# Attention scores by whole 128-key products instead of 64-key halves, with the work around them reordered

## The chip, the cores and the metric

The kernel runs on one core of one Trainium2 chip. The metric is device time in microseconds (us) of one launch. Engines are named as the profile names them: PE is the matrix engine and PEld its weight loads, DVE the vector engine, ACT the scalar engine, POOL the general engine, SP the one that issues most DMA transfers.

## The reference

A linear attention with a decay per key dimension (4 batches, 8 heads, 768 steps, head size 48) is followed by a mixture of experts in which some tokens keep the expert of the token before them.

```python
for t in range(S):                       # attention, all batches and heads at once
    cur = einsum('bhd,bhe->bhde', u * k[t], v[t])
    y[t] = einsum('bhd,bhde->bhe', r[t], state + cur)
    state = w[..., None] * state + einsum('bhd,bhe->bhde', k[t], v[t])
...
x = y.transpose(0, 2, 1, 3).reshape(B, S, H * D)          # B=4, S=768, H*D=384
logits, local_gate = x @ w_gate, sigmoid(x @ w_local)     # 8 experts
for b in range(B):
    for s in range(S):
        e = argmax(logits[b, s]) if s == 0 or local_gate[b, s] < 0.5 else prev_e
        prev_e = e
        out[b, s] = softmax(logits[b, s])[e] * (relu(x[b, s] @ w1[e]) @ w2[e])   # F = 1024
```

## The kernel before

The attention is done in 16 items, numbered n: a batch and a pair of heads each, with the two heads of a pair on partitions 0 to 47 and 64 to 111. The 768 steps of an item are six chunks of 128. The terms of an item are:

- `scale` (POOL): `ke`, keys scaled to the end of their chunk; `rw`, decayed receptances; `pd`, the products of receptance and key that the own term (`u`) needs. `keys` (DVE): `kw`, keys divided by the decay.
- `added` (PE): what each chunk adds to the state, into `mp`; `states` (DVE): the scan over chunks, `S`.
- `scores` (PE): keys times receptances within a chunk, three chunks in one PSUM pair of banks (`pair`, of which there are two, taken in turn by `banks`). Each call gives back the DVE product with a mask that writes `am`.
- `own` (PE, then one DVE product with `vT`): the own terms, which open the PSUM tile `y`. `inside` (PE) adds `am` times values to `y`, `before` (PE) adds what the state carries in. ACT then copies `y` to `xT`.
- `turn` (PE transposes, ACT copies): `xT` to token order in `x`, which is written to DRAM after the fourth pair of a batch. `logits` (PE, ACT) and `token_logits` (PE, ACT) follow once a batch, at n = 4, 8, 12 and at n = 5, 9, 13.

The order on each engine is the order of the program, written out by hand in `run` (a manual schedule); the framework adds only the semaphores. One pass of the loop in `run` for item n first turns item n - 2, makes keys, added states and scan of item n, issues POOL's work for item n + 1, finishes item n - 1 with `inside` and `before`, and then starts item n with `scores` and `own`. PE takes its instructions in that order, so an instruction that waits holds up all behind it. The tile `y` has one buffer: `own` of item n may not write it until `before` of item n - 1 is copied out. Of the two pairs of banks, `scores`, `logits`, `turn` and `token_logits` each take the next one, and wait until its last reader is done.

From n = 9 on the routing of the first two batches (`Router`, on DVE with a few PE products and ACT copies) is spread over the same loop; g is 8. What other engines take from it on the way: `router.keys` (PE) reads what `experts_of` wrote, `router.counts` (PE) what `one_hot` wrote, `router.summed` (PE) what `places` and `numbers` wrote.

The scores before are cut in half by keys: for one chunk and head there are two products with 64 keys each, one with all 128 receptances and one, for the later keys, with the last 64 alone. They go to different halves of the array and of the PSUM partitions, and odd chunks swap the halves, so the tokens of odd chunks are stored with swapped halves by the host (`_tokens`) and masked with a swapped mask (`kept`); `ends` and `turn_ends` hold both orders. The mask product of the second half of the scores is kept back: `run` calls it (`keep()`) behind `own`, except at n = 4, 8, 12, where it comes ahead of it.

The experts follow from about 116 us on. They are not touched, but for the name of a buffer whose memory they take over (`hs`).

Of the kernel before, what the change touches and what calls it, by code (L numbers as in the profile page):

```python
# [61 lines left out]
class Attention:  # L62
# [12 lines left out]

    def __init__(self, tc, st, rk_d, kv_d, vT_d, x_d, w_t, wp_d, kept, ident, lt, mp):
        self.tc, self.nc = tc, tc.nc
        nc = tc.nc
        self.rk_d, self.kv_d, self.vT_d, self.x_d = rk_d, kv_d, vT_d, x_d
        self.w_t, self.kept, self.ident, self.lt = w_t, kept, ident, lt  # L80

# [57 lines left out]

        self.end = once.tile([P, HP, P + DP], F32, name="end")  # L140
        self.endT = once.tile([P, 2, HP, 2 * DH], F32, name="endT")
        self.align(26)
# [23 lines left out]
    def ends(self, z):  # L166
        self.nc.scalar.copy(self.end[:, z, :P], self.tab[:, z, 0, P - 1::-1])
        self.nc.scalar.copy(self.end[:, z, P:], self.tab[:, z, 0, P - 1:DP - 1:-1])  # L168

    def turn_ends(self, z):  # L170
        ep, n = self.banks("ep"), z.stop - z.start
        for k in range(n):
            for o in range(2):
                self.nc.tensor.transpose(ep[:, o, k * P:(k + 1) * P], self.end[:, z.start + k, o * DP:o * DP + P], self.ident)
        self.nc.scalar.copy(self.endT[:, :, z].rearrange("p o i (h d) -> p o (i h) d", h=2),
                            ep[:, :, :n * P].rearrange("p o (i d) -> p o i d", d=DP)[..., :DH])

# [30 lines left out]
    def scale(self, n):  # L208

        nc, t = self.nc, self.items[n]  # L210
        t["ke"] = self.two.tile([P, NCH, 2 * DH], F32, name="ke")
        t["pd"] = self.two.tile([P, NCH, P], F32, name="pd")
        t["rw"] = self.three.tile([P, NCH, P], F32, name="rw")
        hp = t["hp"]

        def ke(p):
            nc.gpsimd.tensor_mul(t["ke"][:, p::2], t["k"][:, p::2], spread(self.endT[:, p, hp], 1, C2))  # L217

        def pd(i):
            z = slice(i * C2, (i + 1) * C2)  # L220
            nc.gpsimd.tensor_mul(t["pd"][:, z], t["rT"][:, z], t["kT"][:, z])  # L221

        def rw(i):
            self.decayed(nc.gpsimd, n, slice(i * C2, (i + 1) * C2))


        for what in (ke, rw, pd) if n > 2 else (pd, ke):
            for i in range(2):
                what(i)
# [32 lines left out]
    def own(self, n):  # L262

        nc, t = self.nc, self.items[n]
        t["y"] = y = self.py.tile([P, 2, 512], F32, name="y")
        for p in range(2):
            for h in range(2):
                q = slice(h * DP, h * DP + DH)
                nc.tensor.matmul(y[p * DP:(p + 1) * DP, h, :C2 * P].rearrange("p (c t) -> p c t", c=C2),
                                 lhsT=self.w_t[q, t["hp"], 1:2].to_broadcast([DH, DP]),  # L270
                                 rhs=t["pd"][q].rearrange("p (c k) t -> p k c t", k=2)[:, p],
                                 start=True, stop=True)
        nc.vector.tensor_mul(y[:, :, :C2 * P], y[:, :, :C2 * P], t["vT"].rearrange("p h c t -> p h (c t)"))

    def scores(self, n, g):
# [5 lines left out]
        for i in range(3):  # L281
            c = 3 * g + i
            for o in range(2):
                for h in range(2):
                    q, f = slice(h * DP, h * DP + DH), c % 2 ^ o

                    x = o * DP if n else 0
                    nc.tensor.matmul(sc[f * DP:(f + 1) * DP, h, i, x:], lhsT=t["kw"][q, c, o * DP:(o + 1) * DP],  # L288
                                     rhs=t["rw"][q, c, x:], start=True, stop=True)
        return lambda: nc.vector.tensor_mul(t["am"][:, g], sc, spread(self.kept[:, g:g + 3], 1, 2))  # L290

    def inside(self, n):
        nc, t = self.nc, self.items[n]
        for c in range(NCH):
            p, c2 = c % 2, c // 2
            for h in range(2):
                nc.tensor.matmul(t["y"][p * DP:(p + 1) * DP, h, c2 * P:(c2 + 1) * P],  # L297
                                 lhsT=t["v"][:, (2 * c + h) * DH:(2 * c + h) * DH + DP],
                                 rhs=t["am"][:, c // 3, h, c % 3], start=False, stop=False, skip_group_check=True)

    def before(self, n):
        nc, t = self.nc, self.items[n]
        if t["hp"] == 0:
            self.xTs[t["b"]] = self.late.tile([P, H, C2 * P], F32, name="xT")
            self.xs[t["b"]] = self.late.tile([P, NCH, D], F32, name="x", bufs=2)
        for c in range(1, NCH):
            p, c2 = c % 2, c // 2
            for h in range(2):
                q = slice(h * DP, h * DP + DH)
                nc.tensor.matmul(t["y"][p * DP:p * DP + DH, h, c2 * P:(c2 + 1) * P],  # L310
                                 lhsT=t["S"][q, :, c - 1], rhs=t["rw"][q, c],
                                 start=False, stop=True, skip_group_check=True)
        for h in range(2) if n == B * HP - 1 else (slice(0, 2),):
            (nc.vector.tensor_copy if h == 1 else nc.scalar.copy)(  # L314
                self.xTs[t["b"]][:, 2 * t["hp"]:2 * t["hp"] + 2][:, h], t["y"][:, h, :C2 * P])

    def turn(self, n, banks):

        nc, b, h0 = self.nc, self.items[n]["b"], 2 * self.items[n]["hp"]
        xT, x = self.xTs[b], self.xs[b]  # L320
        for h in range(2):
            for c2 in range(C2):
                nc.tensor.transpose(banks[h][:, c2 * P:c2 * P + U], xT[:U, h0 + h, c2 * P:(c2 + 1) * P], self.ident[:U, :U])
        for h in range(2):
            nc.scalar.copy(x[:, :, (h0 + h) * DH:(h0 + h + 1) * DH],
                           banks[h][:, :C2 * P].rearrange("p (c e) -> p c e", e=DP)[..., :DH])
        if h0 == H - 2:
            nc.scalar.dma_start(out=self.x_d[b * S:(b + 1) * S, :].rearrange("(c p) d -> p c d", p=P), in_=x)

    def logits(self, b, bank):  # L330
# [3 lines left out]
        for h in range(H):  # L334
            j = h % 4
            nc.tensor.matmul(bank[32 * j:32 * j + 32, :C2 * P], lhsT=self.wp[:, h], rhs=xT[:, h], start=(h < 4), stop=(h >= 4))
        nc.scalar.copy(lT, bank[:, :C2 * P])
# [7 lines left out]
    def run(self, router, fetch, heads):  # L345
# [11 lines left out]
        for n in range(M + 1):  # L357
# [71 lines left out]
            if n == g + 6:  # L429
                router.numbers(0)  # L430
            if n == M:
                router.shares(0)
# [19 lines left out]
            self.scores(n, 0)()  # L452
            keep = self.scores(n, 1)
            if n == g + 1:
                router.experts_of(0, (1,))
            if n == g + 3:
                router.one_hot(0, (1,))
            if n == g + 5:
                router.places(0, 0)
            if n == g + 6:  # L460
                router.places(0, 1)
            if n % HP == 0:

                keep()
                self.own(n)
                self.logits(n // HP - 1, pair("lp")[0])
                if n == g + 4:
                    router.ranks(0, (1,))
            else:
                self.own(n)  # L470
                keep()
            if n == g + 2:
# [4 lines left out]
def general_attention(tc, rk_d, kv_d, wu, wg_d, x_d, ident, lt):  # L477

    nc = tc.nc
    with tc.tile_pool(name="g1", bufs=1) as g1, tc.tile_pool(name="g2", bufs=2) as g2, \  # L480
# [4 lines left out]
        for i in range(2):  # L485
            nc.vector.memset(ones[i * DP:(i + 1) * DP, i:i + 1], 1.0)
        turned = g1.tile([P, P], F32, name="g_turned")
        nc.vector.tensor_copy(turned[:, :DP], ident[:, DP:])
        nc.vector.tensor_copy(turned[:, DP:], ident[:, :DP])
        with tc.For_i(0, HP, 1) as hp:  # L490
            wu_t = g1.tile([P, 2], F32, name="g_wu")
            nc.sync.dma_start(out=wu_t, in_=wu[bass.ds(hp, 1)].rearrange("o p x -> (o p) x"))
            with tc.For_i(0, B, 1) as b:
# [11 lines left out]
                for e in range(DH):  # L505
                    vp = gps.tile([P, 2, 512], F32, name="g_vp")
                    for c in range(NCH):
                        for i in range(2):
                            nc.tensor.matmul(
                                vp[i * DP:(i + 1) * DP, c // 3, (c % 3) * P:(c % 3 + 1) * P],  # L510
                                lhsT=v_t[:, c, i, e:e + 1].to_broadcast([P, DP]),
                                rhs=turned if c % 2 else ident,
                                start=True, stop=True)
# [451 lines left out]
class Experts:  # L965
# [397 lines left out]
    def run(self, att, flag, ready):  # L1363
# [40 lines left out]
        for i in range(n):  # L1404
# [3 lines left out]
            if i == EARLY:  # L1408
                self.fetch(i + 1, self.nc.sync)
                self.hs = self.spare.tile([P, 2, 3, BLOCKS[0] // 2], F32, name="hs", tag="xT")  # L1410
            if u["eleven"]:
# [150 lines left out]
def kernel(  # L1562
# [25 lines left out]

    kept = keep.tile([P, 4, P], F32, name="kept")
    lo, hi = slice(0, DP), slice(DP, P)  # L1590
    nc.gpsimd.tensor_copy(kept[:, 0], mask)
    nc.gpsimd.memset(kept[lo, 1, lo], 0.0)
    nc.gpsimd.tensor_copy(kept[lo, 1, hi], mask[lo, lo])
    nc.gpsimd.tensor_copy(kept[hi, 1, lo], mask[hi, hi])
    nc.gpsimd.memset(kept[hi, 1, hi], 1.0)
    nc.scalar.copy(kept[:, 2:], kept[:, :2])
    lt = keep.tile([P, NC, E + 1], F32, name="lt")
# [6 lines left out]
    with ExitStack() as st, tc.manual_schedule():  # L1604
# [3 lines left out]
        ex = Experts(tc, st, x_d, w1, w2, out, ident, router)  # L1608
        att = Attention(tc, st, rk_d, kv_d, vT_d, x_d, w_t, wp_d, kept, ident, lt, router.mp)
        att.run(router, lambda: ex.fetch(0, nc.sync), lambda: ex.gather(0))  # L1610
# [52 lines left out]
def _tokens(a, np):  # L1663

    x = a.reshape(B, HP, 2, NCH, 2, DP, DH)
    x = np.stack([x[:, :, :, c, ::-1 if c % 2 else 1] for c in range(NCH)], 2)
    return x.transpose(0, 1, 4, 5, 2, 3, 6).reshape(B, HP, P, NCH * 2 * DH)

# [36 lines left out]
```

## Time and profile before

| what | value |
|---|---|
| three runs | 387.30, 389.34, 390.62 us; median 389.34 |
| the profiled execution | 388.15 us, with a span of 386.4 us |
| granted clock of PE | 0.997 |
| busy share of the span | PE 96%, PEld 85%, DVE 64%, POOL 39%, ACT 28% |
| instructions | PE 3858 products and as many loads, DVE 718, ACT 293, POOL 212 |
| attention | first scores at 7.45 us, last carried-in products at 115.53 us |
| mask products (L290) | 32 of 952 ns |
| DMA | 74.97 MB, mean 194 GB/s |

The span runs from the first to the last instruction; 1.75 us of the execution lie around it. A row of a timeline gives the start, the time from the first start to the last end of the instructions it gathers, the engine, the line, the operation, out<-in, the shape and the count, and in brackets the idle time of that engine just before with what ended it ("issue" where the profile shows nothing that it waited for). Each product of 32-bit values is recorded as two products and two loads. PE's starts are measured, its ends are modelled.

### The profile page before, as it was taken

The numbers are of one execution on the slowest core, as the hardware profiler recorded it, in microseconds if no ns is written. First come the engines' busy times: TensorE is split into PE (matmuls) and PEld (weight loads), VectorE is DVE, ScalarE is ACT, GpSimd is POOL, SyncE is SP. The second block draws the span as 40 slices with busy tenths as digits, with TensorE's granted clock in tenths as the row PEclk, the third lists the DMA queues.
The fourth block names the chain that finished last, engine by engine and source line by source line (L and its number), as shares of the span: only waits on it lengthen the run. The fifth ranks groups of instructions, "written<-read, shape, count | busy, mean of one in ns | idle before, by whom it ended". The sixth has DMA issues, their size and how long they took to land. (4 is left out here: it accounts for less than half of the span.)

```text
span 386.4 us, 9723 instructions
## 1 busy us (share of the span) xinstructions
PE 371.5 (96%) x3858; PEld 328.5 (85%) x3858; DVE 247.1 (64%) x718; ACT 107.6 (28%) x293; POOL 151.1 (39%) x212
## 2 busy tenths in 40 slices
PE   7999999799999999999999999999999999999992
PEld 6776877677777999998999999999999999999971
DVE  7887576588954564587657757758757758556400
ACT  4132232222213111322323233234224234222220
POOL 8769998696322022611333222312403213012022
PEclk9999999999999999999999999999999999999998
DMA  7999998979213982740552145245156146064011
GB/s 257 414 409 410 409 405 274 355 256 394 99 32 101 378 338 64 249 185 23 184 179 108 42 170 213 66 171 204 56 185 224 38 165 227 21 199 181 2 37 37
DMA packets 17477, 74.97 MB, mean 194 GB/s; under 512 B 2729, under 2 KB 6586, under 8 KB 14864
## 3 DMA queue, kind: packets, MB, share of 16 engines
q1 hardware_dynamic: 10048, 56.89, 39.1%
q0 software_dynamic: 3424, 9.52, 7.4%
q10 hardware_dynamic: 3952, 7.87, 5.6%
q8 instruction: 32, 0.52, 0.6%
q14 instruction: 21, 0.17, 0.1%
HBM read 64.83 MB, written 9.51 MB: 192 GB/s over the span
## 5 line engine op out<-in xcount | busy, mean ns | idle before, releaser
L1263 POOL DMA_INDIRECT out_dram<-yo,sid x27 | 26.6, 986 | 102.3 <-ACT yo L1258 78.8
L1114 PE MATMUL h<-exT,w1t 128*128 128x168 f32 (+4 forms) x240 | 54.9, 327 | 0.0
L1118 DVE TENSOR_TENSOR hT<-h,hs 128x168 f32<-128x168 f32 (+3 forms) x60 | 21.1, 351 | 46.5 <-PE h L1114 30.4
L1037 POOL DMA_INDIRECT xg<-x_d,gid x29 | 31.1, 1073 | 38.2 <-DVE sm L872 17.4
L1114 PEld LDWEIGHTS h<-exT,w1t 128*128 128x128 f32 x240 | 41.7, 190 | 0.3 <-issue 0.3
L290 DVE TENSOR_TENSOR am<-pair,kept 128x768 f32<-128x768 f32 x32 | 30.1, 952 | 16.8 <-PE pair L288 16.4
L1064 PE MATMUL h<-exT,w1t 128*128 128x192 f32 (+1 forms) x192 | 38.2, 337 | 0.0
L1183 PE MATMUL y<-factors,sums 128*128 128x192 f32 x168 | 36.8, 326 | 0.0
L1114 PE MATMUL h<-xs,ws 128*128 128x168 f32 (+4 forms) x144 | 35.2, 326 | 0.0
L1064 PEld LDWEIGHTS h<-exT,w1t 128*128 128x128 f32 x192 | 32.3, 190 | 1.4 <-issue 0.2
L221 POOL TENSOR_TENSOR pd<-rk 128x384 f32<-128x384 f32 x32 | 31.9, 1017 | 3.0 <-DMA rk<-in_rk_dram 2.2
L297 PE MATMUL y<-am,kv 128*64 128x128 f32 x384 | 28.9, 278 | 3.4 <-issue 2.2
L1114 PEld LDWEIGHTS h<-xs,ws 128*128 128x128 f32 x144 | 25.5, 190 | 4.3 <-ACT hs L1121 1.2
L1183 PEld LDWEIGHTS y<-factors,sums 128*128 128x128 f32 x168 | 28.9, 190 | 0.0
L297 PEld LDWEIGHTS y<-am,kv 128*64 128x64 f32 x384 | 24.8, 136 | 4.7 <-issue 2.4
L234 POOL TENSOR_TENSOR rw<-rk,tab 128x384 f32<-128x384 f32 x26 | 23.6, 931 | 7.3 <-PE y L310 7.3
L217 POOL TENSOR_TENSOR ke<-kv,endT 128x288 f32<-128x288 f32 x32 | 24.9, 799 | 3.9 <-DMA kv<-in_kv_dram 3.0
L314 ACT COPY xT<-y 128x768 f32<-128x768 f32 (+1 forms) x16 | 12.5, 779 | 42.3 <-PE y L310 42.3
L288 PE MATMUL pair<-rw,kw 48*64 48x128 f32 (+1 forms) x768 | 22.4, 249 | 1.3 <-ACT end L168 0.6
L1183 PE MATMUL y<-w2t,hT 128*128 128x192 f32 x96 | 23.0, 328 | 0.0
L1051 DVE COPY exT<-tp 128x384 f32<-128x384 f32 (+6 forms) x29 | 14.0, 489 | 12.8 <-PE tp L1050 12.6
L288 PEld LDWEIGHTS pair<-rw,kw 48*64 48x64 f32 x768 | 19.4, 133 | 2.7 <-issue 0.9
(279 smaller groups left out, 733.0 us busy)
## 6 DMA issues: line engine op xcount, KB each, us to landing
w1t<-in_w_dram SPq DMA_DIRECT2D x9, 1536.0 KB, 6.7
w2t<-in_w_dram SPq DMA_DIRECT2D x9, 1536.0 KB, 7.3
rk<-in_rk_dram SPq DMA_DIRECT2D x15, 768.0 KB, 9.4
kv<-in_kv_dram SPq DMA_DIRECT2D x16, 584.0 KB, 9.1
vT<-in_vT_dram SPq DMA_DIRECT2D x16, 384.0 KB, 7.4
x_d<-x ACTq DMA_DIRECT2D x4, 1152.0 KB, 10.7
w1t<-in_w_dram ACTq DMA_DIRECT2D x1, 1536.0 KB, 10.2
w2t<-in_w_dram ACTq DMA_DIRECT2D x1, 1536.0 KB, 13.5
```

The lines of the kernel that those rows point to most:

```text
L217: nc.gpsimd.tensor_mul(t["ke"][:, p::2], t["k"][:, p::2], spread(self.endT[:, p, hp], 1, C2))
L221: nc.gpsimd.tensor_mul(t["pd"][:, z], t["rT"][:, z], t["kT"][:, z])
L234: engine.tensor_mul(t["rw"][:, z], t["rT"][:, z], spread(pw, 1, z.stop - z.start))
L288: nc.tensor.matmul(sc[f * DP:(f + 1) * DP, h, i, x:], lhsT=t["kw"][q, c, o * DP:(o + 1) * DP], rhs=t["rw"][q, c, x:], start=True, stop=True)
L290: return lambda: nc.vector.tensor_mul(t["am"][:, g], sc, spread(self.kept[:, g:g + 3], 1, 2))
L297: nc.tensor.matmul(t["y"][p * DP:(p + 1) * DP, h, c2 * P:(c2 + 1) * P], lhsT=t["v"][:, (2 * c + h) * DH:(2 * c + h) * DH + DP], rhs=t["am" ...
L1037: self.nc.gpsimd.indirect_dma_start(out=xg[:n], out_offset=None, in_=self.x_d[:rows], in_offset=bass.IndirectOffsetOnAxis(ap=u["gid"][:n, ...
L1064: nc.tensor.matmul(h[:, :n], lhsT=u["w1"][:, m, kk, :], rhs=u["xT"][:, kk, :], start=(kk == 0), stop=(kk == DK - 1))
L1114: nc.tensor.matmul(out, lhsT=a, rhs=b, start=start and k == 0, stop=stop and k == len(terms) - 1, skip_group_check=True)
L1118: nc.vector.tensor_tensor(out, a, b, op=Alu.add)
L1183: return lambda: nc.tensor.matmul(bank[:, x * half:(x + 1) * half], lhsT=a, rhs=b, start=(j == 0 and x == 0), stop=(j == FK // 2 - 1), ski ...
L1263: self.nc.gpsimd.indirect_dma_start(out=out.rearrange("n (h d) -> (n h) d", h=2) if half else out, out_offset=bass.IndirectOffsetOnAxis(ap ...
```

## The change

1. **Scores.** For a chunk and a head there is one product: 128 keys by 128 receptances. The array is then used as two halves by rows (the two heads) in place of four quarters. The swapped order, `kept` and the second order of `end` and `endT` go; the mask is broadcast over three chunks and two heads.
2. **Order of an item from n = 3 on.** `scores` first half and its mask product, `own`, `scores` second half and its mask product, then `logits` where it is due. Items 0 to 2 keep their order.
3. **One tile a head.** `y` becomes `y0` and `y1`, `xT` becomes `xT0` and `xT1`. `own` goes through the heads outside and the halves inside, and its DVE product becomes two, one a head. The copy of `y` to `xT` is now split for every item: head 0 by ACT, head 1 by DVE (before, only the last item did this).
4. **Routing.** `experts_of` (second part, n = 9), `one_hot` (second part, n = 11) and `places` come behind the second mask product; before, they stood between the second scores and `own`, which on DVE is between the first mask product and the product of `own`. `places` of the first half moves from n = 13 to n = 14, and that of the second half from n = 14 to n = 15, there ahead of `inside`.

```diff
@@ own
-        t["y"] = y = self.py.tile([P, 2, 512], F32, name="y")
-        for p in range(2):
-            for h in range(2):
+        t["y"] = y = [self.py.tile([P, 512], F32, name=f"y{h}") for h in range(2)]
+        for h in range(2):
+            for p in range(2):
...
-        nc.vector.tensor_mul(y[:, :, :C2 * P], y[:, :, :C2 * P], t["vT"].rearrange("p h c t -> p h (c t)"))
+        for h in range(2):
+            nc.vector.tensor_mul(y[h][:, :C2 * P], y[h][:, :C2 * P], t["vT"][:, h].rearrange("p c t -> p (c t)"))
@@ scores
-            for o in range(2):
-                for h in range(2):
-                    q, f = slice(h * DP, h * DP + DH), c % 2 ^ o
-                    x = o * DP if n else 0
-                    nc.tensor.matmul(sc[f * DP:(f + 1) * DP, h, i, x:], lhsT=t["kw"][q, c, o * DP:(o + 1) * DP],
-                                     rhs=t["rw"][q, c, x:], start=True, stop=True)
-        return lambda: nc.vector.tensor_mul(t["am"][:, g], sc, spread(self.kept[:, g:g + 3], 1, 2))
+            for h in range(2):
+                q = slice(h * DP, h * DP + DH)
+                nc.tensor.matmul(sc[:, h, i], lhsT=t["kw"][q, c], rhs=t["rw"][q, c], start=True, stop=True)
+        return lambda: nc.vector.tensor_mul(t["am"][:, g], sc, spread(spread(self.mask, 1, 3), 1, 2))
@@ before
-        for h in range(2) if n == B * HP - 1 else (slice(0, 2),):
+        for h in range(2):
             (nc.vector.tensor_copy if h == 1 else nc.scalar.copy)(
-                self.xTs[t["b"]][:, 2 * t["hp"]:2 * t["hp"] + 2][:, h], t["y"][:, h, :C2 * P])
+                self.xTs[t["b"]][h][:, t["hp"]], t["y"][h][:, :C2 * P])
@@ run
             if n == g + 6:
                 router.numbers(0)
+            if n == g + 7:
+                router.places(0, 1)
...
             self.scores(n, 0)()
-            keep = self.scores(n, 1)
+            self.own(n)
+            self.scores(n, 1)()
+            if n % HP == 0:
+                self.logits(n // HP - 1, pair("lp")[0])
             if n == g + 1:
                 router.experts_of(0, (1,))
             if n == g + 3:
                 router.one_hot(0, (1,))
-            if n == g + 5:
+            if n == g + 4:
+                router.ranks(0, (1,))
+            if n == g + 6:
                 router.places(0, 0)
-            if n == g + 6:
-                router.places(0, 1)
-            if n % HP == 0:
-                keep()
-                self.own(n)
-                self.logits(n // HP - 1, pair("lp")[0])
-                if n == g + 4:
-                    router.ranks(0, (1,))
-            else:
-                self.own(n)
-                keep()
@@ ends, turn_ends (one order in place of two), and in the kernel itself
-        self.nc.scalar.copy(self.end[:, z, :P], self.tab[:, z, 0, P - 1::-1])
-        self.nc.scalar.copy(self.end[:, z, P:], self.tab[:, z, 0, P - 1:DP - 1:-1])
+        self.nc.scalar.copy(self.end[:, z], self.tab[:, z, 0, P - 1::-1])
-    kept = keep.tile([P, 4, P], F32, name="kept")
...
-    nc.scalar.copy(kept[:, 2:], kept[:, :2])
```

`inside` and `turn` do the same instructions on the new tiles, `ke` in `scale` takes contiguous chunks, and general code for unusual decays (not run here) follows the new order of tokens.

## The prediction

> **What bounds the kernel now.** I read the page first, then the waits of PE, then the timeline, since the change touches the attention alone (7 to 116 us).
>
> ```profile
> span 386.4 us, 9723 instructions
> PE 371.5 (96%) x3858; PEld 328.5 (85%) x3858; DVE 247.1 (64%) x718; ACT 107.6 (28%) x293; POOL 151.1 (39%) x212
> ...
> q8 instruction: 32, 0.52, 0.6%
> ...
> L290 DVE TENSOR_TENSOR am<-pair,kept 128x768 f32<-128x768 f32 x32 | 30.1, 952 | 16.8 <-PE pair L288 16.4
> ```
>
> No engine is visibly the bound: PE's 96% counts overlapping modelled ends, and DVE, 64% busy, waits 16.4 us for scores. So I followed one plain item, n = 7.
>
> ```profile
> 52.56 0.25 PEld L310 LDWEIGHTS y<-rw,S 48*48 48x48 f32 x4 [0.17 <-issue]
> 53.16 0.48 PEld L310 LDWEIGHTS y<-rw,S 48*48 48x48 f32 x16 [0.36 <-issue]
> 53.68 1.19 PE L288 MATMUL pair<-rw,kw 48*64 48x128 f32 x48
> 53.92 0.80 ACT L314 COPY xT<-y 128x768 f32<-128x768 f32 x1 [2.91 <-PE y L310]
> 54.48 0.96 DVE L290 TENSOR_TENSOR am<-pair,kept 128x768 f32<-128x768 f32 x1 [1.57 <-PE pair L288]
> 54.87 0.88 PE L269 MATMUL y<-pd,w_t 48*64 48x384 f32 x8
> 55.86 0.97 DVE L273 TENSOR_TENSOR y<-y,vT 128x768 f32<-128x768 f32 x1 [0.42 <-PE y L269]
> 56.73 0.95 DVE L290 TENSOR_TENSOR am<-pair,kept 128x768 f32<-128x768 f32 x1
> ```
>
> The loop closes through two engines: `before` ends (the copy at 53.92 marks it), scores, first mask product (54.48), a wait for `own` (0.42), the product of `own` (55.86), second mask product (56.73), then on PE the second half of `inside`, `before`, and the next copy at 60.12. The copies (L314) give each item's length: they start at 27.74 (n = 3), 33.51, 41.80, 47.73, 53.92, 60.12, 67.96, 76.38, 82.48, 88.62, 96.34, 102.63, 109.85 and 115.85.
>
> Two kinds of pause belong to PE itself:
>
> ```profile
> PEld y L310 <- issue: 3.1, 16, 0.4
> PEld y L297 <- issue: 2.4, 1, 2.4
> ...
> PEld pair L288 <- issue: 0.6, 1, 0.6
> ```
>
> Of the 0.19 us mean ahead of `before`, 0.17 recurs in every item: it is where the array goes from 128x64 weights (`inside`) to 48x48. The others, 0.36 twice, 0.5 (33 us) and 2.16 (72 us), together 3.4 us, have no releaser. I take them for waits for instructions: 32 transfers of 16 KB carry PE's 7716 records, some 240 each, and a plain item has about 250.
>
> **The change on PE.** These rows of n = 11 give the lengths:
>
> ```profile
> 84.23 0.59 PEld L323 LDWEIGHTS pair<-ident,xT 112*128 112x128 f32 x6 [0.60 <-DVE am L290]
> 84.96 0.53 PEld L253 LDWEIGHTS mp<-kv,ke 128*48 128x48 f32 x20
> 85.55 0.30 PEld L716 LDWEIGHTS mp<-oh,r_ones 128*128 128x128 f32 x2
> 86.16 1.58 PE L297 MATMUL y<-am,kv 128*64 128x128 f32 x24
> 87.67 0.79 PE L310 MATMUL y<-rw,S 48*48 48x128 f32 x18
> ```
>
> *Scores.* In `inside` 24 records take 1.58 us on two column halves: less a modelled last record of 0.27, a pair takes 1.31 / 12 = 0.109 us, its 64-column loads hidden. A score product of 128 keys runs on two row halves, so half the scores (12 records) take 6 x 0.11 = 0.66 us. The nearest row for a load of 128 columns, L342 (six in 0.74 us, 0.11 each after the first 0.19), does not raise that. Before, both halves took from 53.68 to 54.87 less the modelled tail, about 1.0. Not shown is whether two row halves load 128 columns at once. If they don't, half the scores take 12 x 0.11 = 1.32. But before, sixteen loads of 64 columns took 0.35 us (48 in 1.13 at n = 8, less one of 0.13, average 0.021 each); two column halves one after the other by rows, at half of 0.11 each, would need 0.44. So the rows overlap, and I take 0.66.
>
> The page "TensorE: Matmul & The Clock Gate" of the Trainium skill (Part 3, The mechanism) says that a load overlaps a running product only where the row group differs. By it each half would show load plus product, 6 x 0.22 = 1.32 us, and the sum below would be 1.3 us an item longer. The rows of `inside`, all on the same rows, contradict it.
>
> *Changes of shape.* `before` uses quarters, scores now row halves, `own` quarters, scores again row halves, then `turn` the whole array: four changes where one was. Bounds: 0 (a weight load already prefetched) and 0.17 (row L310). I take 0.13, nearer to the row, since part of it is the ordinary step of 0.05.
>
> The page "TensorEngine Tiling (Array Packing)" (Key Properties) says that a change of tiling mode drains the engine. It gives no time; by it the lower bound of 0 falls, and the sum keeps 0.13 to 0.17.
>
> *A plain item from the copy's start:* scores started 0.24 before it (53.68 against 53.92); now 0.13 later, and half of them end at 0.55. `own` waits for the copies of `y`: ACT's half is 0.48 (its row at 115.85), DVE's half 0.49 (L1051, 128x384), so 0.57; with the change of shape 0.68. Its 8 records take 0.65 (0.88 less the tail): 1.33. Second scores end at 1.33 + 0.13 + 0.66 = 2.12, `turn` starts at 2.25, `added` 0.73 later (84.23 to 84.96), `inside` 0.59 after that (84.96 to 85.55), the next copy 2.46 after that (86.16 to 88.62): 6.03, say 6.05. With shape changes at 0: 5.66; at 0.17: 6.2. Before: 6.20, of which 0.36 was a pause.
>
> **The change on DVE.** First mask product at 0.56 + 0.16 + 0.13 = 0.85 (half the scores grows from 0.50 to 0.66). Starts of 768-element products follow 0.86 apart; two of 384 cost 2 x 0.465 (L241 halves) = 0.93 against 0.87. With `own` done at 1.55 the wait of 0.42 is gone: second mask product at 0.85 + 0.86 + 0.93 = 2.64, free at 3.5, seen at 3.6. `inside` starts at 3.57 and needs it 0.66 later: hidden, so PE now sets the plain item and the removed wait buys nothing. The DVE copy (0.46) fits between 0.04 and 0.85; if scores came sooner it would cost at most 0.2. ACT loses 0.3 to it and is idle there.
>
> **Items with more.**
>
> - n = 8 (and 4, 12): `logits` now follow the second scores: 2.25, `turn` 1.42 later (61.87 to 63.29), 3.67 against 3.17 before: +0.5. `turn` also waits for the second mask product, 3.65: no more.
> - n = 9: `experts_of` (0.6) comes behind it, so PE's `router.keys` waits until 3.5 + 0.6 + 0.07 = 4.17; 0.2 to `inside`, then 2.46: 6.83. Behind the waiting transpose stand `inside`, `before` and the scores.
> - n = 10: `turn_runs` and `last`, 0.16 and 0.32, no longer in a wait: 6.53.
> - n = 11: `router.counts` waits for `oh`: 3.5 + 0.52 + 0.07 = 4.09, then 0.61 and 2.46: 7.16.
> - n = 14: `places` 0.87, keys 0.86, scan 0.57 and, in the next item, `places` 0.95 all stand ahead of `router.summed` on PE: 3.5 + 3.25 + 0.07 = 6.82, plus 1.74 (108.11 to 109.85) = 8.56.
> - Start: three transposes fewer (0.33) against 0.15 to 0.3 at n = 1 and 2, where scores still stand ahead of `own`: +0.1. `kept` costs POOL and ACT nothing that was waited for: POOL waits for DVE's `w` anyway.
>
> POOL issues no transfer sooner; SP's loads are the same, AHEAD stays.
>
> **Sum**, after minus before: start +0.1; n = 3: 6.05 - 5.77 = +0.28; n = 4: 8.36 (n = 8 + 0.5) - 8.29 = +0.07; n = 5 to 7: +0.12, -0.14, -0.15; n = 8: +0.5; n = 9: 6.83 - 8.42 = -1.59; n = 10: +0.43; n = 11: 7.16 - 6.14 = +1.02; n = 12: +0.5; n = 13: 6.05 - 6.29 = -0.24; n = 14: 8.56 - 7.22 = +1.34; n = 15: 0. Together +2.24, without any pause for instructions. These stay: 48 records fewer an item, 770 in all, are three of some 18 transfers; 3.4 x 15 / 18 = 2.8. So 388.15 + 5.0 = 393.2 for an execution like the profiled one. That one lies 1.2 under the median of the runs; runs differ by about one long pause, so I add half of it: **393.8 us**, 1.1% over 389.34. I count 1% (3.9 us) as what a measurement here can tell.
>
> **Rivals.**
>
> - *Shape changes cost nothing (not slower).* Place: PE from `before` to `turn`; price 0 instead of 0.13; it decides if scores to `turn` take 2.1 us or less. Ten items save 0.39: 393.8 - 3.9 = 389.9. For it: the 0.17 may be the semaphore of `inside`. Against: it recurs sixteen times. Chance 0.20.
> - *Pauses for instructions vanish.* For: there are fewer records in a microsecond, so each transfer has longer. 393.8 - 2.8 = 391.0. Chance 0.14. With the rival above 387.1, and below 385.4 only if `logits` hide too: 0.09.
> - *Row halves don't load at once.* +0.66 twice an item, 15 items: +20, 414; against it the loads counted above. Chance 0.07.
> - The forecast: 0.50, its own range 391.5 to 399 (0.17 a change +1.8, pauses doubled +3.4).
>
> Range 387 to 399. Faster by over 1%: 0.09; within: 0.20 + 0.14 = 0.34; slower: 0.50 + 0.07 = 0.57.
>
> **What would show it.** Right: plain items of 6.0 us, no wait of DVE for `own`, PE idle ahead of L679, L716 and L790 at about 70, 85 and 108 us. Wrong: second mask product still the last release of `inside`; scores of 1.3 us a half; items under 5.8 us.

## The result and the profile after

| | runs | median | lowest to highest |
|---|---|---|---|
| before | 9 | 389.0 us | 387.3 to 390.79 |
| after | 9 | 391.62 us | 391.52 to 392.23 |

The ratio is 1.0078, with a 95% interval of 1.0055 to 1.01: slower, by under 1%. On a second chip it was 1.0083 (1.0054 to 1.0112; run `after_same` below). Ratios leave out runs that lie over 1.5% above the fastest of their kernel; where a range of runs is given, it holds all. The profiled execution of after took 391.52 us, with a span of 389.8.

The page of after, in the lines that answer to those of before:

```profile
span 389.8 us, 8966 instructions
PE 376.8 (97%) x3470; PEld 331.4 (85%) x3470; DVE 255.3 (66%) x749; ACT 101.8 (26%) x290; POOL 149.8 (38%) x207
...
q8 instruction: 29, 0.48, 0.5%
...
L286 DVE TENSOR_TENSOR am<-pair,mask 128x768 f32<-128x768 f32 x32 | 30.4, 952 | 3.8 <-PE pair L285 3.6
```

PE issues 388 products fewer, and the mask products, which waited 16.4 us for scores, wait 3.6. Yet the span is 3.4 us longer. The timeline of n = 7 shows what an item is now (rows of PE, ACT and DVE; weight loads, POOL, transfers and what is not used here are left out):

```profile
54.75 0.94 PE L285 MATMUL pair<-rw,kw 48*128 48x128 f32 x12
54.86 0.48 ACT L310 COPY xT<-y 128x384 f32<-128x384 f32 x1 [2.04 <-PE y L306]
54.90 0.56 DVE L310 COPY xT<-y 128x384 f32<-128x384 f32 x1 [0.99 <-PE y L306]
55.62 0.88 PE L268 MATMUL y<-pd,w_t 48*64 48x384 f32 x8
55.74 0.96 DVE L286 TENSOR_TENSOR am<-pair,mask 128x768 f32<-128x768 f32 x1 [0.28 <-PE pair L285]
56.43 0.94 PE L285 MATMUL pair<-rw,kw 48*128 48x128 f32 x12
56.61 1.02 DVE L273 TENSOR_TENSOR y<-y,vT 128x384 f32<-128x384 f32 x2
57.30 0.79 PE L319 MATMUL pair<-ident,xT 112*128 112x112 f32 x6
57.54 0.95 DVE L286 TENSOR_TENSOR am<-pair,mask 128x768 f32<-128x768 f32 x1
58.02 0.66 PE L252 MATMUL mp<-kv,ke 128*48 128x48 f32 x20
58.51 1.50 PE L293 MATMUL y<-am,kv 128*64 128x128 f32 x24
59.93 0.90 PE L306 MATMUL y<-rw,S 48*48 48x128 f32 x20
```

PE's rows follow one another without a wait to the next copy at 60.86. `inside` (L293) runs through: 1.50 us for 24 products. In n = 5 to 7 of before it took 1.94, since its second half waited for the second mask product. It also takes its products in a new order now, the two chunks of a head one after the other; where nothing held it up before (n = 2, 4, 11, 12) it took 1.55 to 1.58, so that up to 0.08 can be the order. DVE goes from the first mask product through `own`'s product to the second without one. Item lengths, between starts of ACT's copy (after: L310):

| n | 1 | 2 | 3 | 4 | 5 | 6 | 7 | 8 | 9 | 10 | 11 | 12 | 13 | 14 | 15 |
|---|---|---|---|---|---|---|---|---|---|---|---|---|---|---|---|
| before | 6.25 | 7.49 | 5.77 | 8.28 | 5.94 | 6.19 | 6.20 | 7.84 | 8.42 | 6.10 | 6.14 | 7.72 | 6.29 | 7.22 | 5.99 |
| predicted | | | 6.05 | 8.36 | 6.05 | 6.05 | 6.05 | 8.34 | 6.83 | 6.53 | 7.16 | 8.22 | 6.05 | 8.56 | 5.99 |
| after | 6.62 | 7.85 | 6.04 | 8.34 | 6.01 | 6.01 | 6.00 | 8.34 | 7.44 | 6.62 | 7.00 | 8.35 | 6.01 | 8.33 | 5.97 |

The last copy starts 3.06 us later than before (118.91 against 115.85), the first transposes of the experts 2.60 later, and at 150 us PE loses 0.78 more. The waits from 20 to 118 us (engine, what waits, for whom: total, times, longest):

```profile
PEld pair L285 <- issue: 7.8, 13, 0.6
...
PEld y L306 <- issue: 2.4, 14, 0.2
...
PEld pair L332 <- issue: 1.2, 6, 0.2
...
PE mp L667 <- DVE key L660: 1.0, 1, 1.0
PE mp L778 <- DVE S L258: 0.8, 1, 0.8
DVE y L273 <- PE y L268: 0.8, 1, 0.8
...
PE mp L704 <- DVE oh L695: 0.2, 1, 0.2
```

The waits on L667, L704 and L778 are the three that the prediction named as its sign. The three rows with `issue` are short and come again and again; the largest is the weight loads of the second scores, idle while the products of `own` run. A long one that comes once, as the 2.4 us of before, is not in the list: PE has no pause for instructions. That is the step of the prediction that failed; most of the experiments are about it.

### The profile page after: what moved, and what is told of

Read it like the earlier page. It is cut to its first block, busy times and chain, and to the rows that moved or that the text cites. A ratio compares the mean times of both kernels' runs of the same rounds, so it can differ in the third digit from the quotient of the medians.

```text
span 389.8 us, 8966 instructions
## 1 busy us (share of the span) xinstructions
PE 376.8 (97%) x3470; PEld 331.4 (85%) x3470; DVE 255.3 (66%) x749; ACT 101.8 (26%) x290; POOL 149.8 (38%) x207
## 5 line engine op out<-in xcount | busy, mean ns | idle before, releaser
L285 PEld LDWEIGHTS pair<-rw,kw 48*128 48x128 f32 x384 | 24.0, 187 | 10.9 <-issue 8.1
L286 DVE TENSOR_TENSOR am<-pair,mask 128x768 f32<-128x768 f32 x32 | 30.4, 952 | 3.8 <-PE pair L285 3.6
L285 PE MATMUL pair<-rw,kw 48*128 48x128 f32 x384 | 29.8, 289 | 0.4 <-DVE rw L233 0.3
L293 PE MATMUL y<-am,kv 128*64 128x128 f32 x384 | 25.0, 276 | 0.4 <-DVE am L286 0.2
L293 PEld LDWEIGHTS y<-am,kv 128*64 128x64 f32 x384 | 21.0, 137 | 1.4 <-DVE y L273 0.5
L1102 PE MATMUL h<-xs,w1t 128*128 128x168 f32 (+4 forms) x96 | 19.7, 328 | 0.0
```

The lines of the kernel that those rows point to most:

```text
L285: nc.tensor.matmul(sc[:, h, i], lhsT=t["kw"][q, c], rhs=t["rw"][q, c], start=True, stop=True)
L293: nc.tensor.matmul(t["y"][h][p * DP:(p + 1) * DP, c2 * P:(c2 + 1) * P], lhsT=t["v"][:, (2 * c + h) * DH:(2 * c + h) * DH + DP], rhs=t["am" ...
L1102: nc.tensor.matmul(out, lhsT=a, rhs=b, start=start and k == 0, stop=stop and k == len(terms) - 1, skip_group_check=True)
```

## Experiments

Each ratio is to runs of the kernel before on the same chip. Its median there was 389.4 us for `after_own_last` and `before_ahead3` and 386.8 to 387.0 for all others, so times that were expected from its 389 are read as differences. "Record k" counts all records of PE in the trace in order: products, weight loads, and those of its sequencer, most of them semaphores (129 in before).

### The parts of the change, one at a time

**Scores alone** (`keys128_only`): the kernel before with only the new scores, mask and token order.

```diff
-            for o in range(2):
-                for h in range(2):
-                    q, f = slice(h * DP, h * DP + DH), c % 2 ^ o
...
+            for h in range(2):
+                q = slice(h * DP, h * DP + DH)
+                nc.tensor.matmul(sc[:, h, i], lhsT=t["kw"][q, c], rhs=t["rw"][q, c], start=True, stop=True)
```

> The kernel before with the scores of 128 keys alone; own behind both halves, one tile for y and xT, and the routing stay as in the kernel before. Theory (the longer scores are on the path, since own, its product and the second mask product follow them): own starts 0.45 to 0.5 us later after the copy, a plain item goes from 5.84 (6.20 less its pause of 0.36) to about 6.3, 15 times about +0.45 is +6.8, less the pauses that go (2.8): 393. Rival (the longer scores lie in time in which PE waits for the product of own): items of 5.9, and with the pauses gone 386 to 387.

Measured: 390.36 us (five runs within 0.11 us), ratio 1.0081 (1.005 to 1.0112); plain items 6.26. The theory had the item, and nearly the sum: 393 was +4 us, the ratio is +3.1. Its timeline, n = 7, copy at 55.46:

```profile
56.88 0.88 PE L268 MATMUL y<-pd,w_t 48*64 48x384 f32 x8
57.88 0.97 DVE L272 TENSOR_TENSOR y<-y,vT 128x768 f32<-128x768 f32 x1 [0.59 <-PE y L268]
58.91 1.94 PE L292 MATMUL y<-am,kv 128*64 128x128 f32 x24
```

`own` starts 1.42 us after the copy (0.95 before), its product at 2.42 (1.94 before), and `inside` takes 1.94 again: the longer scores are paid in full on the old chain over DVE.

**Order of `own`** (`after_own_last`): the changed kernel with `own` behind both halves.

```diff
             self.scores(n, 0)()
-            self.own(n)
-            self.scores(n, 1)()
+            keep = self.scores(n, 1)
+            if n % HP == 0:
+                keep()
+                self.own(n)
+            else:
+                self.own(n)
+                keep()
```

> The changed kernel with own behind both halves of the scores, and the second mask product behind the product of own (ahead of own at n = 4, 8, 12), as in the kernel before; scores of 128 keys, split tiles and copies, and the place of the routing stay as changed. Theory (PE sets the plain item, so the order of its pieces is worth only one change of array shape, 0.17 to 0.2 us): plain items 5.85 in place of 6.01, about 389 beside 390.8. Rival (with own later, the chain own, its product, second mask product, second half of inside decides again): own starts 0.6 us later, the second mask product ends about 4.25 us after the copy, PE needs it at 4.1, items of 6.1 to 6.25 as in keys128_only (6.26), 391 to 392; then it is the order of own, not the split copies, that brought 6.26 down to 6.01.

Measured: ratio 1.0167 (1.012 to 1.0215), from four of eight runs, which lie from 395.7 to 403.2. The profiled execution ran at half clock from 75 to 92 us, so only its items up to n = 7 are read: 6.29, 6.29 and 6.30 for n = 5 to 7. The rival holds for the items; both times are missed. Beside 6.26 for the scores alone, tiles and copies by head bring nothing to a plain item; `own` between the halves brings the 0.28 from 6.29 to 6.01. What these runs lost after that is open.

**Scores of 64 keys in the new order** (`keys64`):

```diff
-                nc.tensor.matmul(sc[:, h, i], lhsT=t["kw"][q, c], rhs=t["rw"][q, c], start=True, stop=True)
+                    nc.tensor.matmul(sc[f * DP:(f + 1) * DP, h, i, x:], lhsT=t["kw"][q, c, o * DP:(o + 1) * DP],
+                                     rhs=t["rw"][q, c, x:], start=True, stop=True)
```

> The changed kernel with the scores, masks and token order of the kernel before (products of 64 keys on four quarters); own between the halves, tiles by head and routing stay as changed. Theory (PE sets the plain item, and each half of the scores costs it 0.87 us with 128 keys): 48 records went in 1.19 us before, so a half takes about 0.6, a plain item goes from 6.01 to about 5.5, the three with logits likewise, the routed ones less; some 12 times -0.5, about 385.5. Rival (with shorter scores the chain over DVE sets the item again): plain items stay at 5.9 to 6.0, 391. Third (pauses for instructions belong to the number of records, and an item has 48 more again): items at 5.5 but single gaps on PE of 0.4 to 2.4 us at every 256th record, together up to 2.8 us, 388, and runs that differ by 3 us again instead of by 0.7.

Measured: 390.25 us, runs from 389.36 to 393.24, ratio 1.0092 (1.0058 to 1.0126). The undisturbed plain item, n = 13, takes 5.56, as the theory said: PE does set the plain item of after, and 128 keys cost it 0.45. But the third theory holds too, on the pauses and the spread, though the time is longer than its 388. In the waits:

```profile
PE y L311 <- issue: 1.6, 1, 1.6
```

Its gaps stand at records 1217 (0.94 us), 1729 (0.34) and 1985 (1.86), each 193 above a multiple of 256. After the third the granted clock was at half for 7 us, and n = 7 took 8.34. From its windows (stretch, then busy time of PE, PEld, DVE, ACT, POOL; the last three are clock, DMA share, GB/s):

```profile
54.00:56.00 2.00, 1.11 (x34) 1.11 (x35) 0.34 (x1) 0.38 (x1) 2.00 (x3) 0.86 0.99 385
56.00:58.00 2.00, 2.00 (x32) 1.48 (x29) 1.29 (x3) 0.10 (x1) 2.00 (x4) 0.50 0.94 379
```

**Routing put back** (`routing_back`): the changed kernel, routing between the first mask product and `own`.

```diff
             self.scores(n, 0)()
+            if n == g + 1:
+                router.experts_of(0, (1,))
+            if n == g + 3:
+                router.one_hot(0, (1,))
+            if n == g + 5:
+                router.places(0, 0)
+            if n == g + 6:
+                router.places(0, 1)
             self.own(n)
```

> The changed kernel with its routing steps put back to where the kernel before has them, between the first mask product and the product of own; all else as changed. Theory (the steps behind the second mask product make PE wait, because the key, oh and ohq that PE reads come later): the item n = 9 goes from 7.44 to about 6.2 us, n = 11 from 7.00 to 6.4, n = 14 from 8.33 to 7.8, while n = 13 grows from 6.01 to 6.5, since places now delays the product of own there; together about -1.9 us, 389.7. Rival (PE sets every item, so DVE's order is nothing): within 0.5 us of the changed kernel, 391.6, items as they are. Second rival (the steps delay the product of own as much as they delayed PE): n = 9, 11, 13 and 14 all above 6.8, and 392 or more.

> The changed kernel once more, unchanged, as the measure for the three runs beside it: 1.0055 to 1.01 of the kernel before, runs within 1 us of each other, no pause of PE for instructions.

Measured: 390.77 us, ratio 1.0093 (1.0057 to 1.013), against 390.80 and 1.0083 for `after_same`, on another chip. The last copies start at 118.88 and 118.90: nothing gained, nothing lost. n = 11 falls from 6.99 to 6.76 and n = 14 from 8.33 to 7.71, but n = 13 grows from 6.01 to 6.57 and n = 9 from 7.43 to 7.63. The theory falls. The first rival has the time, but the items do move; the second has the cause (what PE gains, the product of `own` loses), but not its sizes, since n = 11 and n = 13 stay under 6.8 and the time under 392. In n = 9 three small steps of `experts_of` that I put at 0.6 us took 2.0:

```profile
70.97 0.24 DVE L658 TENSOR_REDUCE k<-eq 128x12 f32<-128x96 f32 x1
71.06 1.96 POOL L220 TENSOR_TENSOR pd<-rk 128x384 f32<-128x384 f32 x2
71.24 0.83 DVE L659 TENSOR_TENSOR k<-t,k 128x12 f32<-128x12 f32 x1
...
72.11 0.93 DVE L660 SCALAR_TENSOR_TENSOR key<-lt,k 128x12 f32<-128x12 f32 x1
```

Both products end when a product of POOL ends: at 72.08 and 73.04, POOL's two at 72.05 and 73.02. In after, L660 at 73.24 took 0.75 and ended at 73.99, POOL's `ke` at 73.97. In before the two took 0.17 and 0.18, from 69.57 on, as one row of POOL ended (69.69) and before the next began (69.95). In `after_own_last` the two take 0.77 and 0.71 and end at 75.22 and 75.96, POOL's at 75.19 and 75.94. No run took POOL away, so this is read from five coincidences.

### The pauses for instructions

The trace has the start of each 16 KB transfer of PE's instructions (q8). In before, from 28 to 80 us, PE passes a block end (record 193 above a multiple of 256) and the next transfer starts 3.6 to 6.0 us later; where PE waits, the first record of the new block comes 2.3 to 2.5 us after that. Together this is as long as, or longer than, the 5.8 to 6 us that 256 records of plain items take. At 104 us, with DMA nearly idle, the transfer starts after 0.7 us. In after a block lasts 7.1 us and more, the transfers start 0.7 to 3.9 us after a block end, and they come in time. Why they start sooner there, with DMA as busy (1.02 and 409 GB/s from 28 to 42 us in both), is open.

**Records shifted** (`before_shift66`): the kernel before, filler products at the start fewer and wider.

```diff
-        self.align(26)
-        self.warm(8)
+        self.wide(4)
+        self.wide(3)
...
-        self.warm(5)
+        self.wide(1)
```

> The kernel before with the filler products at the start made wider and fewer (9 of 384 columns for 42 narrower ones), about 66 records fewer at nearly the same length; nothing else. Theory (PE's instructions come in blocks of 256 records, and the pauses stand where a block ends: records 1217, 1729, 1985, 2241 and 2753 of the kernel before are all 193 above a multiple of 256): the gaps stay at records 193 above a multiple of 256, which are 66 records later in the program, in the own products of n = 7 and 8 and the scores of n = 10; time from -1.5 to +0.5 us against the kernel before, since some of them now lie in time in which PE waits anyway. Rival (the pause of 2.4 us belongs to its place or its time, 72 us): the gap stays in inside of the tenth item at 72 us, and the time within 0.3 us.

Measured: 389.75 us, ratio 1.0074 (1.0044 to 1.0105), runs from 388.61 to 392.11. The shift came out as 100 records (7616 products and loads for 7716), not 66, and the filler was not of equal length: the first copy starts at 16.07 for 14.00, which is 2.1 us of the loss. The gaps are now at records 1217 (0.83), 1729 (1.03) and 3265 (0.60), all still 193 above a multiple of 256, and at other instructions; the one of 2.4 us at 72 us is gone. So they belong to the count of records, not to a place in the program; which blocks have one varies.

**Smaller loads** (`before_rows96`, `after_rows96`, `keys64_rb_rows96`): `rk` and `vT` without their unused partitions.

```diff
-        if n:
+        if n >= AHEAD:
+            for q in (slice(0, DH), slice(DP, DP + DH)):
+                nc.sync.dma_start(out=rk[q].rearrange("p a c t -> p (a c t)"), in_=self.rk_d[b, hp][q])
+        elif n:
...
-        nc.sync.dma_start(out=vT.rearrange("p a c t -> p (a c t)"), in_=self.vT_d[b, hp])
+        for q in (slice(0, DH), slice(DP, DP + DH)) if n >= AHEAD else (slice(0, P),):
+            nc.sync.dma_start(out=vT[q].rearrange("p a c t -> p (a c t)"), in_=self.vT_d[b, hp][q])
```

> The kernel before, with the loads of rk and vT from the fifth item on cut to the 96 partitions that are used (two transfers of 48 rows instead of one of 128): 1448 KB an item for 1736. Theory (a block of 256 records is asked for when PE enters the one ahead of it, but its transfer stands behind the item loads: in the kernel before it starts 3.6 to 6.0 us after that between 34 and 78 us, 0.7 us at 104 us where DMA is 16 percent busy; with the 2.3 us from its start to the first record this is more than the 6.1 us in which PE goes through a block, so PE waits): with less traffic the transfers start sooner, the pauses at records 193 above a multiple of 256 shrink from 3.4 us in all to under 1.5, time from -1 to -3 us against the kernel before, and its runs lie closer than 3 us. Rival (records in a microsecond alone decide): transfers and pauses as before, time within 0.5 us.

> The changed kernel with the same smaller loads. Theory (its blocks last 7.4 us and come in time already, and PE sets its items): within 0.5 us of the changed kernel beside it, items of 6.0. Rival (less traffic helps every item, for instance by loads that come late): 1 to 3 us below the changed kernel, as much as for the kernel before.

> The changed kernel with scores of 64 keys, with routing where the kernel before has it, and with the smaller loads. Theory (the records of the scores cost PE 0.45 us an item less, and the pauses and the slow clock that followed one of 1.9 us were what ate it): plain items of 5.6 us from n = 5 on, no pause above 0.5 us, 4 to 6 us below the changed kernel beside it and 1 to 3 below the kernel before. Rival (shorter items need their blocks sooner, 250 records in 5.6 us, so pauses stay): gaps of 0.5 to 2 us at every 256th record, within 2 us of the changed kernel.

Measured: ratios 1.033 (1.0278 to 1.0382), 1.0296 (1.024 to 1.0352) and 1.0366 (1.0264 to 1.0469), the last from two of six runs, which lie from 398.85 to 413.21. All times expected failed: with the smaller transfers, stretches in which DMA is as busy as before move little over half to two thirds of the bytes in a microsecond. Each load also became two; which of the two does it is not shown. `after_rows96`, windows and then waits from 28 to 80 us:

```profile
28.00:42.00 14.00, 13.00 (x196) 9.24 (x190) 10.31 (x18) 2.86 (x8) 11.61 (x19) 1.00 1.03 232
```

```profile
POOL ke L220 <- DMA kv<-in_kv_dram: 12.1, 8, 4.1
...
PE pair L289 <- issue: 1.4, 1, 1.4
...
PE y L310 <- issue: 1.0, 1, 1.0
PE mp L256 <- issue: 1.0, 1, 1.0
PE y L297 <- issue: 1.0, 1, 1.0
```

In the same stretch the kernel of after moved 409 GB/s. The miss is worth more than the hit would have been: in the changed kernel, which had no pause, four gaps of 1.1 to 1.7 us appear, at records 961, 1217, 1473 and 2241, all 193 above a multiple of 256. Their transfers started 5.8 to 6.8 us after PE had passed a block end. So few records do not protect by themselves; the delay of the transfer under item loads counts as much.

**Order of the loads** (`before_kv_last`, `keys64_rb_kv_last`): from the fifth item on, `kv` behind `vT`.

```diff
+        if n < AHEAD:
             nc.sync.dma_start(out=kv, in_=self.kv_d[b, hp])
         nc.sync.dma_start(out=vT.rearrange("p a c t -> p (a c t)"), in_=self.vT_d[b, hp])
+        if n >= AHEAD:
+            nc.sync.dma_start(out=kv, in_=self.kv_d[b, hp])
```

> The kernel before with one line moved: from the fifth item on the load of kv is issued behind that of vT, not ahead of it; bytes and shapes stay. Theory (the transfer of PE's instructions waits until the item loads issued before it are through: rk and kv are issued together at 46.5 and 46.9, 52.4 and 52.8, 58.6 and 59.0 us, 1352 KB or 3.3 us at 410 GB/s, right when PE enters a block and asks for the next, at 47.0, 53.2 and 59.4; vT follows 4 us later, and the instructions start at 50.8, 57.0 and 63.5, just as rk and kv are through): now only rk, 1.9 us, stands ahead, so the transfers start 1.5 to 2.5 us after PE entered the block in place of 3.6 to 4.2, in time, the pauses of 0.4 to 2.4 us go, and the time falls by 1.5 to 3 us with runs within 1.5 us of each other. Rival (what counts is the amount of traffic or the number of records, not the order): pauses, spread and time as in the kernel before, within 0.5 us.

> The changed kernel with scores of 64 keys, routing where the kernel before has it, and the load of kv behind that of vT from the fifth item on. Theory (in the run of keys64 the pauses and the slow clock after one of them cost 5 us, the items themselves take 5.6; its first score half and own come 0.4 us sooner than in the changed kernel): pauses under 1 us in all, plain items of 5.5 to 5.7 from n = 5 on, 383 to 386, so 5 to 7 us below the changed kernel. Rival (shorter items ask for blocks sooner than they come, whatever the order of the loads): gaps of 0.5 to 2 us at every 256th record as with keys64, 388 to 391 and a spread of 3 us.

Measured: 388.21 us, ratio 1.0025 (1.0006 to 1.0044), and 388.30 us, 1.0033 (1.0012 to 1.0054). The transfers of `before_kv_last` still start 3.6 to 5.2 us late (50.94, 57.52, 63.74) and its pauses stay, so that the place of `kv` in the queue does not set them. The second kernel has n = 5 at 5.57, and pauses of 0.4 to 1.2 us at four block ends up to 59 us, so each of its theories holds in part. It is the best variant of the changed kernel, 2.5 us under `after_same` (on another chip), and still not under before.

**Fewer loads under way** (`before_ahead3`): one item less ahead.

```diff
-AHEAD = 4
+AHEAD = 3
```

> The kernel before with its item loads running one item less ahead (three buffers of rk and vT and four of kv for four and five); the same bytes. Theory (the transfer of PE's instructions stands behind whatever loads are queued, so with fewer queued it starts sooner): from 28 to 55 us DMA is busy under 0.95 in place of 1.02, the instructions start under 3 us after PE enters a block in place of 3.6 to 4.2, the pauses at records 193 above a multiple of 256 fall by half, time -1 to -2 us. Rival (the items go through as many bytes in each 6 us, so DMA is as busy when the instructions are asked for): starts of 3.6 us and more, time within 0.5 us. Third (a load now comes late): POOL waits for rk or kv in items, slower by over 1 us.

Measured: ratio 1.003 (0.9992 to 1.0067), from seven of twelve runs, which lie from 387.67 to 397.67. The theory on the pauses holds, more fully than expected, though DMA is not under 0.95 and the time does not fall. Windows, then waits from 28 to 70 us:

```profile
42.00:55.00 13.00, 13.00 (x273) 9.99 (x265) 9.40 (x12) 3.68 (x13) 13.00 (x18) 1.00 0.97 351
```

```profile
PEld y L310 <- issue: 1.0, 6, 0.2
...
PEld y L269 <- issue: 0.6, 3, 0.2
```

DMA is busy 0.97 and moves 351 GB/s where the kernel before had 1.03 and 410; the transfers start 0.6 to 2.5 us after the block end, no gap over 0.1 us is left at a block end of the attention, and n = 5, 6 and 7 take 5.78, 5.77 and 5.77 for 5.94, 6.19 and 6.20. Up to n = 8 this is the kernel before without its pauses. The third theory takes the gain back: later on loads come late (POOL waits 4.5 us for `kv`), and n = 9, 13 and 15 take 7.19, 9.12 and 7.20. In n = 13 two more things come in: small DVE steps of 0.72 to 0.93 us beside POOL (L730 to L734, from 89.63 on), and a granted clock at half from 99 to 102 us.

## Why the prediction was right, and where it was wrong

The forecast of 393.2 for an execution like the profiled one met 391.52; as a median it was 393.8 against 391.62. The way it moved is right, and the time lies in the range. But "slower by over 1%", with a chance of 0.57, did not come: 0.78% belongs to "within", which had 0.34. By its steps:

- **Row halves load at once: right.** Half the scores takes 0.87 us with its change of shape (54.75 to 55.62) for the 0.66 + 0.13 put down, not 1.32. That rival is out.
- **Changes of shape: a little small.** 0.87 less 0.66 is 0.2, nearer to the row of 0.17 than to the 0.13 taken. Against it, `added` to `inside` took 0.44 where 0.59 was put down (the row at 85.55 is a routing product, L716, not `inside`), and the scores start 0.11 ahead of the copy, not 0.13 behind. That 6.05 came so near to 6.01 is partly luck: such errors evened out.
- **PE sets the plain item: right.** Shorter scores give 5.56 in the same order.
- **"The removed wait buys nothing": wrong as said.** Without pauses a plain item goes 5.77 (`before_ahead3`), 6.26 (scores alone), 6.01 (after). Moving `own` gives back 0.25 to 0.28; the scores take 0.49.
- **Items with logits and routing: right but for n = 9.** Its miss of 0.61 is L660, 0.75 us for 0.18. That moving the routing costs, by itself, is not so: in the changed kernel either place gives the same sum. What the prediction charged to the place is DVE's work, wherever it stands; how much of it is DVE's new copy of `y` was not tried apart.
- **Start: wrong, 0.71 for 0.1.** The transposes saved bought nothing (first copy 13.98 for 14.00). In n = 1 and 2 the longer scores stand ahead of `own`, which starts at 15.76 for 15.40 in n = 1, and cost 0.37 and 0.36 where 0.15 to 0.3 was put down for them. DVE's copy of `y` is not the cause: the kernel with the scores alone has no such copy, and its items take 6.60 and 7.84 (after 6.62 and 7.85).
- **Pauses: wrong, and the largest miss.** "These stay ... 2.8" was the step: I scaled 3.4 us by the number of transfers. PE had none in after. What sets them is the time a block lasts against the delay of its transfer. The rival with this cause said 391.0, at a chance of 0.14. The 0.6 added to the forecast for half a long pause goes with them: the median of after lies 0.1 above its profiled execution.
- **Not foreseen.** In the last item of before, DVE's copy (116.36) stood behind ACT's (115.85) on the one tile `xT`; with a tile a head both run at once: -0.46. And in the experts ACT began an `hT` at 150.25, 4.57 us after the same step of before, where its neighbours stand 2.59 after theirs: 2.0 us late, when the products that the profile names as its releaser had ended at 148.17. What held it is open; PE lost 0.78 in this execution, and the profile of `after_same` does not have it.

From 393.2: -2.8 for the pauses, +0.61 for the start, +0.61 for n = 9, -0.39 for the other items, -0.46 for the last copies, +0.78 for ACT give 391.55; measured are 391.52. The terms are read from the two traces themselves, so that they add up shows only that none is missing. With the pauses alone put right the sum would have said 390.4: the start, n = 9 and the late ACT, none of them foreseen, made up for half of the miss, which is luck. So 0.50 was given to the case whose items came true and whose pauses did not; the time fell between it and the rival, inside the former's own range.

The spread of the runs fits: before varies by 3.5 us over nine runs, after by 0.7. It is no proof, since `before_ahead3` has no pauses and varies by 10.

## What to carry to other kernels

A pause with no releaser that recurs every 256 records is a rate problem: compare the time of one block with the delay of its transfer under the loads of that stage, and do not scale it by the number of transfers. Where an engine is kept off the path by a wait elsewhere, price the move and the longer instruction apart; here one gave 0.28 and the other took 0.49 an item. And before loads are trimmed to fewer partitions, look at the GB/s that they reach.

## What the runs showed of the hardware

- **Instruction transfers.** The Trainium skill, "Runtime: NRT & Kernel Launch" (Instruction fetch mechanics), says that instructions come in 16 KiB blocks of 256 and that crossing a block is mostly hidden. The blocks agree with the gaps at records 193 above a multiple of 256. "Mostly hidden" does not hold under load: 3.4 us in before, 1.1 to 1.7 us a gap in `after_rows96`.
- **The clock.** The granted clock was at half for 6.8 us after a gap of 1.86 us on PE in `keys64`, for 17.1 us from within a wait of 2.4 us on in `after_own_last`, and for 3.4 us after one of 1.55 us in `before_ahead3`; in before a gap of 2.4 us left it at 1.00. "TensorE: Matmul & The Clock Gate" (Part 1, What's actually happening) ties the drop to an idle window of about 3.4 us; here it came with shorter gaps, not every time. That the gaps caused it is read from the order in time alone.
- **DVE beside POOL.** Products of 12 elements, with both inputs in SBUF, took 0.71 to 0.93 us in place of 0.17 while POOL worked. So did steps with one input: a copy of 8 elements (L733) took 0.82 us in `before_ahead3`, with POOL at work, and 0.17 in before, without. "GPSIMD Engine Reference" (Specifications) says that POOL shares its SBUF interfaces with DVE, with contention for DVE instructions that have two SBUF inputs or run in a mode with two ports. The first fits; which mode the copy ran in no run shows.
- **Transfers of 48 partitions.** Stretches with `rk` and `vT` loaded to 48 partitions at a time moved 211 to 283 GB/s with DMA 0.95 to 1.04 busy, where those with 128 moved about 410.
